# An attention and feed-forward kernel: the order of every engine and of the loads fixed by one model

## The chip, the cores, the metric

The kernel runs on one core of a Trainium2 chip. The metric is the time of one execution on the device in microseconds (us), lower is better. Medians are over repeated executions. A profile is of one execution; its span is about 2 us shorter than the time.

## The reference, cut to what matters

```python
def _attn_ref(q, k, v, n_global, n_local):      # 4 batches, 8 heads, 768 rows, 64 wide
    scores = (q @ k^T) / 8
    keep = (column < 8) | (0 <= row - column < 96)     # 8 global columns, a local band of 96
    scores = where(keep, scores - slope[head] * dist, -1e9)
    return softmax(scores) @ v

def _moe_ref(x, w_in, w_out):                   # 3072 rows, 512 -> 2048 -> 512
    h = x @ w_in
    return (h - tanh(h)) @ w_out

def reference(...):
    x = attention output, heads side by side: (3072, 512)
    return _moe_ref(x, w_in, w_out)
```

## The kernel before

The 3072 rows are 24 tiles of 128 rows, six for each batch. Every tile goes through attention (cast to bf16, transpose, scores, exp, product with a mask, product with V, normalization, transpose), then through the input matmuls with w_in (in groups of one or three tiles), tanh and subtraction, and the output matmuls with w_out. Only a band of two 128x128 blocks of scores per tile is computed; the eight global columns are copied into each tile's own K and V. That copy of V, eight partitions tall, is done on GpSimd ("the V copy").

All loads of q, k, v go through the queue of the SyncE engine (tile 0's q alone through ScalarE's), the four quarters each of w_in and w_out through GpSimd's. A planner fixes the order of TensorE, with a guess of when loads land; GpSimd's program is fixed by the place of each call. ScalarE, VectorE and SyncE are ordered by the default scheduler. The parts that the change touches:

```python
    EARLY = 3
    groups = [[0], [1], [2], [3, 4, 5]] + [[u, u + 1, u + 2] for u in range(6, NU, 3)]
    ...
    def cast(u):
        kf, qf, vf = staged.pop(u)
        ...
        eng = nc.vector if u < EARLY else nc.gpsimd
        eng.tensor_copy(out=k_bf, in_=kf.rearrange("p h d -> p (h d)"))
        eng.tensor_copy(out=q_bf, in_=qf.rearrange("p h d -> p (h d)"))
        nc.gpsimd.tensor_copy(out=vb[u % NV][:, :, 0:Dh], in_=vf)
    ...
    def a_AV(u, part):
        ...                                           # the matmuls with V, then:
        if part == 1 and 1 <= i < NQ - 1:             # the V copy
            nc.gpsimd.tensor_copy(out=vb[u % NV][0:G, :, 0:Dh], in_=vb[(u - i) % NV][0:G, :, 0:Dh])
    ...
    PRE = 3
    after = {0: [("in", 0)], 1: [("in", 1)], 2: [("in", 2), ("in", 3)],
             5: [("out", 0), ("out", 1), ("out", 2), ("out", 3)]}

    with tc.manual_schedule(engines={ENG.PE, ENG.Pool}):
        for u in range(PRE):
            load(u)
        build_masks()

        def weights(u):
            for kind, j in after.get(u, []):
                load_w(kind, j, gate=load_dma[u, "kf"])   # issued once tile u's k has landed

        weights(0)
        cast(0)
        for t, c in order:            # the planner's order of TensorE
            if c[0] == "T":           # transposes of tile u
                u = c[1]
                if u + PRE < NU:
                    load(u + PRE)
                if u + 1 < NU:
                    weights(u + 1)
                    cast(u + 1)
            ...
```

The softmax here doesn't subtract the row's maximum and nothing guards it: scores larger than these inputs give would overflow.

## Time and profile before

| | before |
|---|---|
| time, median of 3 (range) | 258.38 us (257.66 to 258.41) |
| profiled span, mean granted clock of TensorE | 256.0 us, 0.998 |
| TensorE busy, by the page | 86% |
| TensorE work done by 60 us / left after it | 26.0 us / 178.3 us |
| last quarter of w_out landed | 55.6 us |

The fourth row is a count of mine. I take the weight loads of each TensorE line up to a moment (there is one for each matmul), each counted once, at its start, and give each what such a matmul costs back to back: 0.163 us for an input matmul of 128x384, 0.109 for 128x256, 0.056 for 128x128, 0.216 for an output matmul, 0.057 for a transpose, 0.030 for the attention's small ones. In sum 204.3 us.

From the page of the kernel before: busy tenths of TensorE and of the DMA engines, and the rate moved, in 40 slices of 6.4 us; then the chain of work that ended last.

```profile
span 256.0 us, 4940 instructions
PE   1107688769999999988998799999998999999994
DMA  8999999999901959915860119811011100211012
GB/s 157 220 210 203 231 205 201 194 221 225 254 31 41 228 145 180 191 42 147 184 123 4 41 60 231 164 41 41 3 41 41 44 4 0 82 44 41 0 44 82
PE 74%; DMA 10%; DVE 5%; ACT 5%; SPq 3%; issue 1%; POOL 0%
```

In the first ten slices (64 us) the DMA engines are full and TensorE is not; in the rest it is the other way about. The longest DMA pieces of the chain (start, duration):

```profile
7.51 10.70 DMA qf<-in_q_dram
...
40.91 14.73 DMA w_out_bf_105<-in_moe_w_out_dram
```

The first is tile 2's q, until 18.2 us. The second is the last quarter of w_out, until 55.6 us. Why the first holds TensorE is seen on VectorE's timeline (start, duration, what; in brackets the idle time before it and what ended it):

```profile
9.26 0.68 DVE L174 COPY qk<-sm 128x1024 bf16<-128x1024 bf16 x1
16.10 0.43 DVE L156 CAST k_bf<-kf 128x512 bf16<-128x512 f32 x1 [6.16 <-DMA kf<-in_k_dram]
18.23 0.43 DVE L157 CAST q_bf<-qf 128x512 bf16<-128x512 f32 x1 [1.71 <-DMA qf<-in_q_dram]
18.57 0.68 DVE L191 TENSOR_TENSOR pd<-pd,mk 128x1024 bf16<-128x1024 bf16 x1
```

The mask product of tile 0 at 18.57 could have run from 11.7 us, when its exp on ScalarE ended; it stands behind the casts of tile 2, which wait for their loads. And TensorE waits for that product (waits of TensorE up to 75 us: in total, times, longest):

```profile
PE op L208 <- DVE pd L191: 9.5, 3, 8.7
```

The steady part, by stretches (columns: length, then busy us and instructions of TensorE, its weight loads, VectorE, ScalarE and GpSimd, the granted clock, the DMA share, GB/s):

```profile
60.00:100.00 40.00, 39.38 (x335) 22.67 (x333) 24.51 (x46) 19.35 (x24) 8.62 (x15) 1.00 0.65 150
100.00:140.00 40.00, 37.78 (x349) 21.57 (x348) 27.15 (x49) 20.59 (x26) 7.75 (x13) 1.00 0.61 123
140.00:180.00 40.00, 37.93 (x329) 21.50 (x328) 24.20 (x49) 16.30 (x22) 11.22 (x19) 1.00 0.42 93
180.00:220.00 40.00, 39.12 (x338) 22.17 (x337) 27.92 (x49) 22.07 (x27) 5.17 (x9) 1.00 0.08 28
```

TensorE's busy time is 154.2 of these 160 us, 96%. The counted work is 147.4 us, 92%. The Trainium skill, "Perfetto Trace Analysis", "Identifying the Most-Contended Engine", says that the busy share of matmuls is a bad measure because matmuls are pipelined, and tells the reader to look at the share of the peak reached and at the weight loads instead.

### The profile page before, as it was taken

To read this page: it belongs to the slowest core of one execution; us is meant where nothing else is said; L and a number is where in the kernel's file an instruction comes from. 1 tells how busy PE (TensorE), PEld (TensorE's weight loads), DVE (VectorE), ACT (ScalarE), POOL (GpSimd) and SP (SyncE) were. 2 spreads that over 40 slices of the span, in tenths; PEclk is the share of its full clock that TensorE was granted. 3 is DMA by queue.
4 is the path that set the end of the run, shared out by engine and by line. 5 is a ranking of instruction groups with operands and counts; after the bars stand their busy time and mean duration, and the time that the engine had idled before them with its cause. 6 is when DMAs were issued, how large, how long until landed. Compare 5 with 4: busy or idle time off the path is not lost.

```text
span 256.0 us, 4940 instructions
## 1 busy us (share of the span) xinstructions
PE 218.9 (86%) x2016; PEld 129.9 (51%) x2016; DVE 148.8 (58%) x286; ACT 113.1 (44%) x145; POOL 57.8 (23%) x107
## 2 busy tenths in 40 slices
PE   1107688769999999988998799999998999999994
PEld 0005577535555556544655366555654556545541
DVE  2223878953774558655668557744785577444710
ACT  5300556702743535651467235722582455234610
POOL 6231239241003327006200244042001500000000
PEclk9999999999999999999999999999999999999999
DMA  8999999999901959915860119811011100211012
GB/s 157 220 210 203 231 205 201 194 221 225 254 31 41 228 145 180 191 42 147 184 123 4 41 60 231 164 41 41 3 41 41 44 4 0 82 44 41 0 44 82
DMA packets 82582, 29.68 MB, mean 116 GB/s; under 512 B 75392, under 2 KB 79488, under 8 KB 82560
## 3 DMA queue, kind: packets, MB, share of 16 engines
q1 hardware_dynamic: 77296, 24.91, 44.8%
q0 software_dynamic: 4224, 4.19, 10.0%
q10 hardware_dynamic: 1040, 0.26, 0.5%
q8 instruction: 16, 0.26, 0.4%
q14 instruction: 6, 0.05, 0.1%
HBM read 27.26 MB, written 6.29 MB: 131 GB/s over the span
## 4 chain that ended last, share of the span: by engine, by line
PE 74%; DMA 10%; DVE 5%; ACT 5%; SPq 3%; issue 1%; POOL 0%
PE big L263 31%; PE op L292 30%; DMA w_out_bf_105<-in_moe_w_out_dram 6%; DMA qf<-in_q_dram 4%; PE big L182 4%; PE sm L173 3%; SPq L143 3%; PE sm L208 2%; PE sm L237 2%; ACT ot L298 2%; ACT pd L190 2%; PE sm L292 1%; PE sm L213 1%; DVE xT L242 1%; DVE pd L191 1%
## 5 line engine op out<-in xcount | busy, mean ns | idle before, releaser
L272 ACT ACTIVATE th<-big 128x768 f32<-128x768 f32 (+1 forms) x68 | 52.5, 773 | 70.1 <-PE big L263 70.1
L275 DVE TENSOR_TENSOR g<-big,th 128x768 bf16<-128x768 f32 x56 | 53.6, 956 | 21.7 <-ACT th L272 21.6
L292 PEld LDWEIGHTS <-g 128*128 128x128 bf16 x384 | 34.1, 97 | 37.5 <-issue 4.1
L298 ACT COPY ot<-op 128x512 f32<-128x512 f32 x23 | 13.5, 586 | 49.6 <-PE op L292 49.5
L190 ACT ACTIVATE pd<-big 128x1024 bf16<-128x1024 f32 x24 | 24.5, 1020 | 12.8 <-PE big L182 12.6
L292 PE MATMUL op<-w_out_bf_102,g 128*128 128x512 bf16 x92 | 23.6, 379 | 2.9 <-ACT ot L298 2.7
L208 PEld LDWEIGHTS <-pd 128*128 128x128 bf16 x192 | 14.0, 98 | 21.7 <-DVE pd L191 10.1
L263 PE MATMUL big<-xT,w_in_bf_98 128*128 128x384 bf16 (+1 forms) x160 | 24.4, 303 | 0.0
L292 PE MATMUL op<-w_out_bf_105,g 128*128 128x512 bf16 x92 | 23.8, 380 | 0.5 <-DVE g L275 0.4
L263 PE MATMUL big<-xT,w_in_bf_101 128*128 128x384 bf16 (+1 forms) x160 | 23.3, 294 | 0.7 <-ACT pd L190 0.7
L292 PE MATMUL op<-w_out_bf_103,g 128*128 128x512 bf16 x92 | 23.7, 380 | 0.3 <-DMA w_out_bf_103<-in_moe_w_out_dram 0.3
L263 PE MATMUL big<-xT,w_in_bf_99 128*128 128x384 bf16 (+1 forms) x160 | 23.3, 294 | 0.4 <-DVE g L277 0.4
L292 PE MATMUL op<-w_out_bf_104,g 128*128 128x512 bf16 x92 | 23.6, 380 | 0.0
L263 PE MATMUL big<-xT,w_in_bf_100 128*128 128x384 bf16 (+1 forms) x160 | 23.3, 294 | 0.2 <-DVE g L277 0.2
L220 DVE RECIPROCAL rden<-sm 128x4 f32<-128x4 f32 x42 | 7.6, 181 | 23.9 <-PE sm L213 21.5
L190 ACT ACTIVATE po<-big 128x1024 bf16<-128x1024 f32 x20 | 20.5, 1024 | 1.7 <-PE big L182 1.5
L191 DVE TENSOR_TENSOR pd<-pd,mk 128x1024 bf16<-128x1024 bf16 x24 | 17.2, 716 | 5.0 <-ACT pd L190 4.7
L242 DVE COPY xT<-sm 128x512 bf16<-128x512 bf16 x24 | 10.2, 423 | 15.8 <-PE sm L237 15.8
L174 DVE COPY qk<-sm 128x1024 bf16<-128x1024 bf16 x24 | 16.5, 687 | 4.6 <-PE sm L173 4.5
L182 PE MATMUL big<-qk 64*128 64x128 bf16 x352 | 16.2, 224 | 3.3 <-DVE qk L174 3.3
L221 DVE TENSOR_TENSOR x<-sm,rden 128x256 bf16<-128x256 f32 x42 | 17.8, 424 | 1.3
L263 PEld LDWEIGHTS <-w_in_bf_101 128*128 128x128 bf16 x160 | 13.7, 98 | 8.4 <-issue 0.8
(105 smaller groups left out, 249.0 us busy)
## 6 DMA issues: line engine op xcount, KB each, us to landing
kf<-in_k_dram SPq DMA_DIRECT2D x24, 256.0 KB, 5.0
vf<-in_v_dram SPq DMA_DIRECT2D x24, 256.0 KB, 4.9
out_dram<-ot SPq DMA_DIRECT2D x24, 256.0 KB, 2.0
qf<-in_q_dram SPq DMA_DIRECT2D x23, 256.0 KB, 4.9
w_in_bf_98<-in_moe_w_in_dram POOLq DMA_DIRECT2D x1, 512.0 KB, 7.6
w_in_bf_99<-in_moe_w_in_dram POOLq DMA_DIRECT2D x1, 512.0 KB, 9.0
w_in_bf_100<-in_moe_w_in_dram POOLq DMA_DIRECT2D x1, 512.0 KB, 6.2
w_in_bf_101<-in_moe_w_in_dram POOLq DMA_DIRECT2D x1, 512.0 KB, 9.3
```

Source lines behind the costliest of these rows:

```text
L174: nc.vector.tensor_copy(out=qk[u], in_=tr)
L182: nc.tensor.matmul(s[:, slot(2 * p + hh), :], qk[ku][r, 1, p, :], qk[qu][r, 0, p, :], start=True, stop=True,)
L190: nc.scalar.activation(e, s, AF.Exp, bias=0.0, scale=scale)
L191: nc.vector.tensor_tensor(out=e, in0=e, in1=mk[:, :, m, :], op=ALU.mult)
L208: nc.tensor.matmul(av[:, h, :], pd[u][:, slot(h0 + h), :], vb[u % NV][:, h0 + h, :], start=True, stop=(i == 0),)
L221: nc.vector.tensor_tensor(out=xs[u][:, h0 : h0 + H // 2, :], in0=av[:, :, 0:Dh], in1=rden.to_broadcast([P, H // 2, Dh]), op=ALU.mult,)
L242: nc.vector.tensor_copy(out=xT[g][:, :, o : o + P], in_=tr)
L263: nc.tensor.matmul(t[:, a, o : o + n], w_in_bf[j][:, c, fo : fo + P], xT[g][:, c, 0:n], start=(c == 0), stop=(c == CD - 1),)
L272: nc.scalar.activation(tv, src, AF.Tanh, bias=0.0, scale=1.0)
L275: nc.vector.tensor_tensor(out=dst, in0=src, in1=tv, op=ALU.subtract)
L292: nc.tensor.matmul(o, gs[g][:, f, t * P : (t + 1) * P], w_out_bf[f // FJ][:, f % FJ, :], start=(f == 0), stop=(f == CF - 1),)
L298: nc.scalar.copy(out=ot, in_=o)
```

## The change

Its intent: make every engine's order fit one model that knows each engine, each PSUM bank, each buffer and the DMA engines, so that no engine stands behind an instruction that cannot start. Four parts, named as in the prediction:

- (a) Order of loads: tiles 0 to 2, w_in0, tile 3, w_in1 to w_in3, w_out0, w_out1, tile 4, w_out2, w_out3, tile 5. Where tile and weight loads alternate, a gate (a wait on the landing of the load two places earlier) holds the next load back.
- (b) The k and q casts of tiles 1 and 2 go from VectorE to GpSimd.
- (c) The first groups are 2, 2, 2 tiles instead of 1, 1, 1, 3.
- (d) ScalarE, VectorE, SyncE, TensorE and GpSimd all follow the model's order.

Two small things go along: tile 0's q is loaded through SyncE's queue, and tile 3's product with V uses another PSUM tile.

```diff
-    EARLY = 3
-    groups = [[0], [1], [2], [3, 4, 5]] + ...
+    groups = [[0, 1], [2, 3], [4, 5]] + ...
...
+    before = [("t", 0), ("t", 1), ("t", 2), ("in", 0), ("t", 3), ("in", 1), ("in", 2), ("in", 3),
+              ("out", 0), ("out", 1), ("t", 4), ("out", 2), ("out", 3), ("t", 5)]
+    for n, it in enumerate(before):
+        if n >= 2 and (it[0] == "t") != (before[n - 1][0] == "t"):
+            gate_of[("ld", "kf", it[1]) if it[0] == "t" else it] = landed(before[n - 2])
...
+        e0 = DVE if u == 0 else POOL
+        op(("ck", u), e0, 0.62, lambda ...: cast(u, "k_bf", ...),
+           after=[("ld", "kf", u)], take=["kb"], give=["kf"])
+        op(("T", u), PE, 0.46, lambda ...: a_T(u),
+           after=[("ck", u), ("cq", u), ...], take=["sm"], give=["kb", "qb"])
... (one such line for each operation: engine, duration, what it follows, buffers taken and given)
     def plan():
-        T_TILE, T_W = 3.5, 3.2
-        (a model of TensorE with guessed landings)
+        (takes, again and again, the operation that can start first; loads share one DMA resource)
...
-    with tc.manual_schedule(engines={ENG.PE, ENG.Pool}):
-        (loads, weights and casts at fixed places of TensorE's order)
+    with tc.manual_schedule(engines={PE, ACT, DVE, POOL, SP}):
+        for t, key in sorted(order, key=lambda x: x[0]):
+            ops[key]["fn"]()
```

## The prediction

> **What bounds the kernel now.** By the page the span is 256.0 us. TensorE is busy 86%, but its records overlap, so I count back-to-back costs from the chain of waits: an output matmul (128x512) takes 0.216 us, an input matmul 128x384 0.163 us and 128x128 0.056 us. All of it is about 83 us of input matmuls, 83 of output matmuls and, as an estimate, 39 of attention: 205 us. The other 51 us are lost:
> - Head. The chain has 25.6 us in two DMA waits: a q load until 18.2 us, and the last quarter of w_out until 55.6 us. The DMA engines are saturated up to 60 us (table by stretches). By then TensorE has done three tiles of input matmuls and 26 of 384 output matmuls: some 26 of the 205 us.
> - Steady state, 60 to 252.5 us: about 179 us of work in 192.5 us; the rest is short steps of ScalarE and VectorE in the chain.
> - Tail, 3.5 us.
>
> **Head, in detail.** The four w_out loads are issued only at 38.7 to 40.9 us, behind about nine tiles of q, k, v, and land between 45 and 56 us, while TensorE starves. VectorE waits 6.2 us for tile 2's k with tile 0's mask product behind it (TensorE waits 8.7 us for that product).
>
> **The change.** The arithmetic stays. (a) Loads are gated into the order tiles 0-2, w_in0, tile 3, w_in1-3, w_out0-1, tile 4, w_out2-3, tile 5. (b) Casts of tiles 1 and 2 leave VectorE for GpSimd, about 0.9 us each; tile 0's attention no longer waits behind a DMA. (c) Groups 1,1,1,3 become 2,2,2: 128x256 input matmuls, estimated 0.109 us between the measured sizes, so TensorE time stays within 1 us. (d) ScalarE, VectorE and store order follow the model instead of the default scheduler.
>
> **Cost.** The DMA part (3) gives a weight quarter 3.2 us (10.0% of the span over 8); a tile costs about 3.45 us in the head. Then w_in3 lands near 29-31 us, w_out1 near 35-37, w_out3 near 45-47, tile 5 near 48-51. The Trainium skill, "DMA: Bandwidth & Descriptors", "Issuing engines are not separate DMA queues", says queues share the same engines and interleave; so ungated tiles slow the weights. The trace agrees: w_out lands 6.8 to 14.7 us after issue. I expect one small bubble: w_in1 sits on GpSimd behind a copy that waits for tile 1's attention.
>
> So by 47 us TensorE should have done four tiles of input matmuls, one of output matmuls and four to five attentions, about 25 us of work, with 10 us of output matmuls ready: from there it is busy. Before, that point came at about 57 us. Gain of the head: 9 to 11 us. Then 180 us of work, plus steady losses of 6 to 12 us (14 now), plus a tail of 3.5 us: span 236 to 242, time about 2.4 us more. Prediction 241 us.
>
> **On the critical path.** Nearly all of (a) and (b); (d) only in part, since TensorE already was 97% busy there; (c) nearly nothing.
>
> **What would show it.** Last w_out landing before 49 us; TensorE idle under 1 us per 20 us from 48 us on; input matmuls of four tiles done by 40 us; output matmuls at 60 us 60 or more (26 before); DMA in the chain under 22 us; steady ScalarE and VectorE shares of the chain halved.
>
> **What would make it wrong.** A load later than the model's, with in-order engines stuck behind it; bubbles at the gates; GpSimd casts too slow for tiles 1-3; the single output bank stalling TensorE; VectorE freeing PSUM late.

## The result, and the profile after

| | before | after |
|---|---|---|
| time, median of 3 (range) | 258.38 us (257.66 to 258.41) | 243.92 us (243.36 to 244.26) |
| profiled span, granted clock | 256.0 us, 0.998 | 242.5 us, 0.990 |
| TensorE work done by 60 us | 26.0 us | 33.5 us |
| work left after 60 us, and time for it before the tail | 178.3 in 192.5 us | 170.5 in 179.0 us |
| DMA pieces of the chain | 10% | 2% |
| last quarter of w_out landed | 55.6 us | 46.4 us |

The ratio of after to before is 0.9446, 95% interval 0.9408 to 0.9484. A ratio here and below is the mean time of one kernel's fast runs over that of the kernel before in the same rounds, so it is not quite the ratio of the medians quoted.

The span shrank by 13.5 us. By the counts of the table: 7.5 us of it is work done earlier (33.5 - 26.0), 5.7 us is less loss after 60 us (14.2 before, 8.5 after), and 0.3 us comes from slightly cheaper matmul shapes (204.0 us of work in all instead of 204.3). The tail is 3.5 us in both.

The page after, the same lines (slices of 6.06 us):

```profile
span 242.5 us, 4763 instructions
PE   1477867999999979999999999999999999999994
DMA  8997998999999998580991161101100101111112
GB/s 157 218 216 114 203 219 130 217 223 210 260 236 232 207 251 205 97 188 31 221 214 46 35 142 43 43 3 43 44 26 19 46 0 46 45 43 46 43 43 87
PE 85%; DVE 5%; ACT 3%; DMA 2%; issue 2%; SPq 1%; POOL 1%; ACTq 0%; POOLq 0%
```

Of the DMA pieces of the chain 2% of the span is left; the two long ones are gone. TensorE works from the second slice. There are two dips in the DMA rate, in the fourth and seventh slice (114 and 130 GB/s). Both are seen on GpSimd's timeline, where a weight load stands behind a V copy that waits for TensorE:

```profile
18.45 0.61 POOL L231 COPY vb_107<-vb_106 8x512 bf16<-8x512 bf16 x1 [4.39 <-PE op L212]
19.01 0.75 POOL L153 DMA_DIRECT2D w_in_bf_99<-in_moe_w_in_dram  x1
...
37.25 0.61 POOL L231 COPY vb_109<-vb_106 8x512 bf16<-8x512 bf16 x1 [10.68 <-PE op L212]
37.81 0.75 POOL L156 DMA_DIRECT2D w_out_bf_104<-in_moe_w_out_dram  x1
```

Tile 0's mask product, at 18.57 us before, now runs as soon as its exp is there, on VectorE:

```profile
8.92 0.69 DVE L196 TENSOR_TENSOR pd<-pd,mk 128x1024 bf16<-128x1024 bf16 x1 [1.83 <-ACT pd L192]
```

The stretches after:

```profile
60.00:100.00 40.00, 37.39 (x396) 24.86 (x397) 29.07 (x57) 20.09 (x24) 15.65 (x24) 1.00 1.08 230
100.00:140.00 40.00, 39.18 (x370) 23.72 (x374) 29.77 (x58) 20.20 (x26) 12.01 (x19) 1.00 0.51 114
140.00:180.00 40.00, 39.54 (x343) 23.11 (x347) 27.55 (x52) 20.15 (x25) 9.29 (x15) 1.00 0.16 46
180.00:220.00 40.00, 39.74 (x319) 23.00 (x322) 22.94 (x40) 18.99 (x24) 1.33 (x2) 1.00 0.09 34
```

Busy time is 155.9 of 160 us, 97%, one point more than before. The counted work rose from 147.4 to 152.1 us. The worst stretch is the first, 0.89 of counted work, less than before (0.95); the others are at 0.95, 0.97 and 1.00 (0.89, 0.91 and 0.94 before).

One thing in the head the prediction had not reckoned with. Here are the first input matmuls of the kernel after on TensorE, 16 at a time:

```profile
20.13 3.22 PE L263 MATMUL big<-xT,w_in_bf_98 128*128 128x256 bf16 x16 [0.63 <-DVE xT L246]
26.33 3.54 PE L263 MATMUL big<-xT,w_in_bf_99 128*128 128x256 bf16 x16
31.90 1.91 PE L263 MATMUL big<-xT,w_in_bf_100 128*128 128x256 bf16 x16 [1.25 <-ACT pd L192]
33.65 1.91 PE L263 MATMUL big<-xT,w_in_bf_101 128*128 128x256 bf16 x16
```

The first two sixteens take 3.22 and 3.54 us, the next two 1.91 (each of these times includes the tail of the last matmul): about half the rate, and 2.9 us lost. The granted clock (third number from the right) tells it for one of them only:

```profile
20.00:24.00 4.00, 3.46 (x24) 2.52 (x24) 0.92 (x3) 0.62 (x1) 3.35 (x5) 1.00 0.94 135
24.00:26.00 2.00, 0.64 (x12) 0.47 (x12) 1.79 (x4) 0.41 (x1) 1.16 (x3) 1.00 1.24 206
26.00:28.00 2.00, 1.93 (x12) 1.45 (x13) 0.90 (x2) 0.00 (x0) 0.57 (x2) 0.56 1.24 206
28.00:30.00 2.00, 2.00 (x14) 1.39 (x11) 0.00 (x0) 0.09 (x1) 0.00 (x0) 0.58 1.22 196
```

The Trainium skill, "TensorE: Matmul & The Clock Gate", Part 1, "The HAM clock gate (the 'warmup' mystery)", says that TensorE runs at half clock until it has been active for about 3.4 us, and that the window is free-running, so that runs differ. The rates agree with it: 3.22 against 1.91. Between the two sixteens TensorE was mostly idle (0.64 us busy in 24 to 26 us).

### The profile page after: what moved, and what is told of

Read it like the earlier page. It is cut to its first block, busy times and chain, and to the rows that moved or that the text cites. A ratio compares the mean times of both kernels' runs of the same rounds, so it can differ in the third digit from the quotient of the medians.

```text
span 242.5 us, 4763 instructions
## 1 busy us (share of the span) xinstructions
PE 217.6 (90%) x1926; PEld 133.8 (55%) x1952; DVE 144.9 (60%) x274; ACT 111.0 (46%) x137; POOL 66.0 (27%) x111
## 4 chain that ended last, share of the span: by engine, by line
PE 85%; DVE 5%; ACT 3%; DMA 2%; issue 2%; SPq 1%; POOL 1%; ACTq 0%; POOLq 0%
PE big L263 35%; PE op L292 32%; PE big L184 5%; PE sm L172 5%; DMA qf<-in_q_dram 2%; PE sm L207 2%; PE sm L239 2%; DVE g L282 2%; ACT ot L302 1%; PE sm L212 1%; PE sm L292 1%; SPq L147 1%; DVE x L225 1%; ACT th L275 1%; POOL q_bf L160 1%
## 5 line engine op out<-in xcount | busy, mean ns | idle before, releaser
L275 ACT ACTIVATE th<-big 128x768 f32<-128x768 f32 (+1 forms) x60 | 51.3, 855 | 84.9 <-PE big L263 83.8
L282 DVE TENSOR_TENSOR g<-big,th 128x768 bf16<-128x768 f32 (+1 forms) x60 | 60.5, 1009 | 25.0 <-ACT th L275 24.7
L192 ACT ACTIVATE pd<-big 128x1024 bf16<-128x1024 f32 x24 | 24.5, 1021 | 11.8 <-PE big L184 11.8
L160 POOL CAST k_bf<-kf 128x512 bf16<-128x512 f32 x23 | 16.4, 712 | 36.7 <-PE sm L172 23.3
L263 PE MATMUL big<-xT,w_in_bf_98 128*128 128x384 bf16 (+1 forms) x144 | 24.6, 321 | 0.6 <-DVE xT L246 0.6
L292 PE MATMUL op<-w_out_bf_102,g 128*128 128x512 bf16 x82 | 23.1, 379 | 2.2 <-ACT ot L302 1.5
L263 PE MATMUL big<-xT,w_in_bf_99 128*128 128x384 bf16 (+1 forms) x144 | 24.8, 324 | 0.0
L302 ACT COPY ot<-op 128x512 f32<-128x512 f32 x23 | 13.5, 588 | 24.1 <-PE op L292 22.4
L263 PE MATMUL big<-xT,w_in_bf_100 128*128 128x384 bf16 (+1 forms) x144 | 23.1, 308 | 1.3 <-ACT pd L192 1.3
L292 PE MATMUL op<-w_out_bf_103,g 128*128 128x512 bf16 x88 | 23.1, 379 | 0.2
L263 PE MATMUL big<-xT,w_in_bf_101 128*128 128x384 bf16 (+1 forms) x144 | 23.1, 308 | 0.1
L292 PE MATMUL op<-w_out_bf_105,g 128*128 128x512 bf16 x87 | 22.7, 379 | 0.5 <-issue 0.2
L292 PE MATMUL op<-w_out_bf_104,g 128*128 128x512 bf16 x85 | 22.5, 379 | 0.7 <-issue 0.5
L207 PEld LDWEIGHTS <-pd 128*128 128x128 bf16 x192 | 14.6, 101 | 7.7 <-DVE x L225 3.8
L263 PEld LDWEIGHTS <-w_in_bf_98 128*128 128x128 bf16 x144 | 14.1, 102 | 8.1 <-issue 0.9
L263 PEld LDWEIGHTS <-w_in_bf_99 128*128 128x128 bf16 x144 | 14.4, 103 | 6.9
L263 PEld LDWEIGHTS <-w_in_bf_100 128*128 128x128 bf16 x144 | 13.7, 98 | 8.2 <-issue 1.2
## 6 DMA issues: line engine op xcount, KB each, us to landing
kf<-in_k_dram SPq DMA_DIRECT2D x24, 256.0 KB, 4.8
qf<-in_q_dram SPq DMA_DIRECT2D x24, 256.0 KB, 4.9
vf<-in_v_dram SPq DMA_DIRECT2D x24, 256.0 KB, 4.8
out_dram<-ot SPq DMA_DIRECT2D x24, 256.0 KB, 2.1
```

The lines of the kernel that those rows point to most:

```text
L160: eng.tensor_copy(out=dst[u], in_=src.pop(u).rearrange("p h d -> p (h d)"))
L192: nc.scalar.activation(pr[u, o], s, AF.Exp, bias=0.0, scale=scale)
L207: nc.tensor.matmul(t[:, h, :], pr[u, 0][:, slot(h0 + h), :], vb[u % NV][:, h0 + h, :], start=True, stop=last,)
L263: nc.tensor.matmul(t[:, a, o : o + n], w_in_bf[j][:, c, fo : fo + P], xT[g][:, c, 0:n], start=(c == 0), stop=(c == CD - 1),)
L275: nc.scalar.activation(h_view(ths[g, f0], g), h_view(hs[g, f0], g), AF.Tanh, bias=0.0, scale=1.0)
L282: nc.vector.tensor_tensor(out=dst, in0=h_view(hs.pop((g, f0)), g), in1=h_view(ths.pop((g, f0)), g), op=ALU.subtract,)
```

## The experiments

The theory after the result had two parts. T1: the head gains because the loads come in the right order (a) and because no VectorE instruction stands behind a load (b). T2: the steady gain is VectorE's and ScalarE's order (d). Rivals: (R1) the loads hardly matter, the fixed orders do it all; (R2) the grouping pays; (R3) the loads do it all and the orders nothing. Twelve kernels ran; all gave correct results. The names beginning with b start from the kernel before, those with u and w from the kernel after, and in those the planner plans anew with the edit, unless the text says otherwise.

The medians are of all runs, the ratios of the fast ones alone: two of the four runs of b_groups and of u_casts and one of the six of w_warm and of w_casts_warm were labelled slow.

| kernel | edit | median us (range) | ratio to before, 95% interval |
|---|---|---|---|
| after | the change | 243.92 (243.36 to 244.26) | 0.9446 [0.9408, 0.9484] |
| b_loads | before, load order (a) | 266.21 (266.08 to 266.72) | 1.0297 [1.0233, 1.0361] |
| b_casts | before, casts (b) | 254.87 (254.60 to 255.14) | 0.9888 [0.9848, 0.9928] |
| b_groups | before, groups (c) | 275.48 (272.12 to 278.20) | 1.0552 [1.0446, 1.0658] |
| u_nogate | after, no gates | 243.80 (243.33 to 244.96) | 0.9434 [0.9369, 0.9498] |
| u_oldorder | after, old load order | 251.40 (249.15 to 252.26) | 0.9732 [0.9684, 0.9781] |
| u_casts | after, old casts | 242.32 (239.30 to 243.56) | 0.9313 [0.9259, 0.9368] |
| u_groups | after, old groups | 244.25 (243.08 to 244.37) | 0.9458 [0.9423, 0.9493] |
| u_default | after, old orders of two engines | 250.87 (250.34 to 251.59) | 0.9694 [0.9622, 0.9766] |
| w_warm | after, dummy matmuls | 242.36 (239.71 to 243.41) | 0.9356 [0.9308, 0.9404] |
| w_casts_warm | u_casts, dummy matmuls | 240.67 (239.19 to 242.95) | 0.9327 [0.9281, 0.9373] |
| u_lateout | after, w_out last | 255.78 (254.75 to 256.25) | 0.9929 [0.9881, 0.9977] |
| u_lateout6 | after, w_out last, tile 6 after it | 239.96 (238.99 to 241.78) | 0.9325 [0.9266, 0.9384] |

### b_loads: the order of loads alone

```diff
-        seq = [("t", 0), ("in", 0), ("t", 1), ("in", 1), ("t", 2), ("in", 2), ("in", 3),
-               ("t", 3), ("t", 4), ("t", 5), ("out", 0), ("out", 1), ("out", 2), ("out", 3)]
+        seq = [("t", 0), ("t", 1), ("t", 2), ("in", 0), ("t", 3), ("in", 1), ("in", 2), ("in", 3),
+               ("out", 0), ("out", 1), ("t", 4), ("out", 2), ("out", 3), ("t", 5)]
...
-    after = {0: [("in", 0)], 1: [("in", 1)], 2: [("in", 2), ("in", 3)],
-             5: [("out", 0), ("out", 1), ("out", 2), ("out", 3)]}
+    after = {2: [("in", 0)], 3: [("in", 1), ("in", 2), ("in", 3), ("out", 0), ("out", 1)],
+             4: [("out", 2), ("out", 3)]}
+    loads = {0: [3], 2: [4], 3: [5, 6]}
(and the gates of the kernel after)
```

> The kernel before with the load order of the change alone (gates as in the change, groups and the scheduler of VectorE and ScalarE as before). My theory: the change gains about 7 us in the head from weights that land 9 us earlier and about 6.5 us in the steady stretch from the order of VectorE and ScalarE; the load order alone should then give 250 to 254 us, last w_out quarter landing by 48 us (55.6 before), attention work done at 20 us still poor because the VectorE casts are as before. Rival 1 (order of engines is all): 257 to 259 us. Rival 2 (grouping is all): 257 to 259 us.

It got slower, 266.21 us, against the 250 to 254 us foretold. TensorE's longest wait up to 75 us:

```profile
PE sm L220 <- POOL vb L233: 9.2, 1, 9.2
```

GpSimd stood 9.8 us at the gated load of w_out2, with a V copy behind it that TensorE needed. Between 30 and 40 us TensorE was busy 2.0 of 10 us, and then worked at half clock. So the order of loads, put into the old queues as I put it, moves the blocked queue from VectorE to GpSimd. How much of the 8 us is my own placement of the loads among GpSimd's instructions this run cannot tell; it shows that the order by itself is no gain, not what a better placing would give.

### b_groups: the groups alone

```diff
-    groups = [[0], [1], [2], [3, 4, 5]] + [[u, u + 1, u + 2] for u in range(6, NU, 3)]
+    groups = [[0, 1], [2, 3], [4, 5]] + [[u, u + 1, u + 2] for u in range(6, NU, 3)]
```

> The kernel before with groups of two tiles alone. My theory: TensorE cost per tile hardly changes and the head is bound by loads, so 256 to 261 us. Rival 2 (fewer, wider matmuls and evictions are what helps): 252 us or less.

Far slower than foretold, 275.48 us, with a wide spread; the two fast runs, 272.1 and 273.7 us, are some 14 us slower than the kernel before. In the profile the first input matmul waits for two tiles, until 32.6 us, and the w_out loads, which hang on TensorE's order, are issued at 43.5 us. But the profile fell on a slow run at a granted clock of 0.944, so I read no sizes from it, and that this is the cause is not shown. By the times alone, R2 falls for the old kernel.

### u_nogate: no gates

```diff
-        g = gate_of.get(key)
+        g = None
```

The plan stays as it is, only the waits on landings go.

> The changed kernel with the planned order of every engine kept, but no gate on any load. My theory: tiles 3 to 6 load ahead of or among the weights, w_out lands 5 us or more later than 46.3 us, and the time rises to 248 to 252 us. Rival 1 (the order of the engines does it, loads hardly matter): 243 to 245 us.

No difference: 243.80 against 243.92 us; the 248 us or more of my theory are refuted. Some weights landed later, since tiles shared the DMA engines with them: the w_out quarters took 7.3 to 18.2 us from issue to landing, 5.4 to 13.0 with gates. That is what the Trainium skill, "DMA: Bandwidth & Descriptors", "Issuing engines are not separate DMA queues", leads one to expect: all queues run on the same engines and interleave. But nothing that TensorE needed was late for it. The gates do nothing here.

### u_oldorder: the old order of loads in the new plan

```diff
-    before = [("t", 0), ("t", 1), ("t", 2), ("in", 0), ("t", 3), ("in", 1), ("in", 2), ("in", 3),
-              ("out", 0), ("out", 1), ("t", 4), ("out", 2), ("out", 3), ("t", 5)]
+    before = [("t", 0), ("in", 0), ("t", 1), ("in", 1), ("t", 2), ("in", 2), ("in", 3),
+              ("t", 3), ("t", 4), ("t", 5), ("out", 0), ("out", 1), ("out", 2), ("out", 3)]
```

> The changed kernel with the load order of before (w_in between the first tiles, all w_out after tile 5), gated so that it is really kept. Theory (an early w_out is what the head gains from): last w_out lands near 50 us or later instead of 46.3, the work done at 60 us falls by 3 to 5 us and the time rises to 247 to 249 us. Rival (as the run without gates suggests, the head of the changed kernel is not bound by loads): 243 to 245 us.

251.40 us: 7.5 us slower than the change, and more than the 247 to 249 us foretold. Work done by 20 us is 2.3 us (3.7 in the change), since w_in0 and w_in1 come ahead of tiles 1 and 2; but by 30 us it is 8.7 (8.4), so the loss comes later: by 60 us it is 24.6 (33.5). Tile 3's k is issued at 23.1 us instead of 13.4, and the input matmuls of tiles 2 and 3 begin at 45.6 us instead of 39.5. And there is a second fault, GpSimd's and then TensorE's:

```profile
51.55 0.62 POOL L163 CAST vb<-vf 128x512 bf16<-128x512 f32 x1 [4.60 <-DMA vf<-in_v_dram]
...
54.85 0.19 PE L212 MATMUL sm<-vb,po 128*128 128x65 bf16 x1 [2.61 <-POOL vb L231]
```

This v is tile 6's. It has no gate, is issued among the w_out loads and lands 16 us later; the plan did not know. Behind it stand the casts of tile 7 and then the V copy (at 54.20) for which TensorE waits. It is the fault that u_lateout below has in a larger form, so the 7.5 us are not the price of the order alone. The old order with tile 6 in the list would part the two; it was not run. The edit also keeps the gates, and this order alternates between tiles and weights more often. R1 holds for the gates of the change; for the order it stays open.

### u_casts and b_casts: the casts, in the new and in the old kernel

```diff
 u_casts, from after:
-        e0 = DVE if u == 0 else POOL
+        e0 = DVE if u < 3 else POOL
 b_casts, from before:
-    EARLY = 3
+    EARLY = 1
```

> The changed kernel with the q and k casts of tiles 1 and 2 back on VectorE, everything planned anew. Theory (the plan matters, not the engine): VectorE casts are shorter (0.43 against 0.61 us) and the plan puts them where their load has landed, so 242 to 246 us. Rival (moving the casts is what frees the first attention): VectorE again sits behind tile 2's load, tile 1's attention slips by several us and the time is 248 us or more.

> The kernel before with one part of the change alone: the q and k casts of tiles 1 and 2 on GpSimd. The order of every other instruction on every engine is unchanged. Theory from the prediction (VectorE, waiting for a load, blocks the first attention): tile 0's mask product follows its exponential at 12 us instead of 18.6, x of tile 0 is transposed by 15 to 16 us instead of 21.6, but the later head still waits for w_out until 55 us, so the end moves by 0 to 3 us: 255 to 258 us. Rival (the freed head is worth much by itself): 250 to 254 us.

In the new kernel nothing is lost with the casts on VectorE again: 242.32 us. The two fast runs, 239.3 and 241.2 us, are 1.4% below the change by the ratio, but the two slow, 243.4 and 243.6 us, lie at its time, so I claim no gain. The planner puts a cast on VectorE behind the mask products that come first, so it blocks nothing.

In the old kernel the casts give 2.6 us against the median of the kernel before in the same rounds (257.51 us), 1.1% by the ratio: 254.87 us, just below the 255 to 258 us of my theory. The comparison of instruction orders shows TensorE's, ScalarE's and the loads' order unchanged, so this is the move of four casts alone. Counted work at 20 us is 4.2 us instead of 0.8, the gain that I had foretold for tile 0; by 60 us it is 28.7 instead of 26.0. A part was lost on the way. GpSimd's timeline of b_casts, and TensorE's wait for it:

```profile
26.66 0.61 POOL L157 CAST q_bf<-qf 128x512 bf16<-128x512 f32 x1 [1.61 <-DMA qf<-in_q_dram]
...
27.91 0.61 POOL L226 COPY vb<-vb 8x512 bf16<-8x512 bf16 x1
```

```profile
PE op L213 <- POOL vb L226: 4.7, 1, 4.7
```

The V copy that TensorE waits for stands on GpSimd behind tile 3's casts, which wait for their loads. The queue that stands behind a load is another now, the fault is the same.

### u_groups: the old groups in the new plan

```diff
-    groups = [[0, 1], [2, 3], [4, 5]] + ...
+    groups = [[0], [1], [2], [3, 4, 5]] + ...
```

> The changed kernel with the first groups 1,1,1,3 again. Theory: grouping is nearly neutral in the changed kernel (242 to 246 us), since both reach the same work by 60 us; it only hurt when put alone into the kernel before, where tile 1 was late. Rival: pairs are needed, 248 us or more.

244.25 us, the same as the change. With the planner the groups are neutral; R2 falls here too.

### u_default: VectorE and ScalarE ordered by the default scheduler

```diff
-    with tc.manual_schedule(engines={PE, ACT, DVE, POOL, SP}):
+    with tc.manual_schedule(engines={PE, POOL, SP}):
```

> The changed kernel with the order of TensorE, GpSimd and the load queue kept, but VectorE and ScalarE ordered by the default scheduler again. My theory: work per microsecond of TensorE from 60 to 220 us falls from 0.96 back to 0.92 and the time rises by 5 to 7 us, to 249 to 251 us. Rival 3 (loads do it all): 243 to 245 us.

250.87 us, as foretold, and 7 us slower than the change: taking VectorE's order out costs as much as half of the whole gain. The comparison of instruction orders shows the orders of TensorE, GpSimd and SyncE unchanged and ScalarE's different by one swap only, so it is VectorE's. The chain that ended last:

```profile
PE 76%; DVE 11%; ACT 6%; DMA 2%; issue 2%; SPq 1%; POOL 1%; ACTq 0%; POOLq 0%
```

VectorE is 11% of the chain, 5% in the change. Work done by 60 us is 31.1 us (33.5 in the change), and from 60 to 220 us it is 147.2 us, the sum of the kernel before (147.4) and not that of the change (152.1). So without VectorE's order none of the steady gain is left in the sum, and 2.4 us of the head's go too. Stretch by stretch it is not the kernel before: from 60 to 100 us it does 0.84 of counted work (before 0.95), after that 0.93 to 0.96 (before 0.89 to 0.94). R3 falls.

### w_warm and w_casts_warm: a warm clock

About 70 dummy matmuls of the identity into PSUM tiles that are written afterwards anyway, where TensorE waits in the head. Core of the edit (results are unchanged by it):

```diff
+    WARM_T = {0: (24, 4), 1: (6, 8), 2: (8, 0)}     # before the transposes of k and q, by tile
+            for _ in range(WARM_T.get(u, (0, 0))[1 - j]):
+                nc.tensor.transpose(tr[u][:, j, 0, :], ident, ident)
...                                                  # likewise before scores, 5 before the first m1
```

> The changed kernel with some 70 dummy matmuls of the identity put into the idle time of TensorE in the first 20 us, results unchanged. Theory: the first 32 input matmuls (0.20 us each instead of 0.109, granted clock 0.56 to 0.58 at 26 to 30 us) run at full rate, TensorE gains 3 us in the head, of which 1 to 3 us reach the end: 241 to 243 us. Rival (hidden behind the waits for loads): 243.5 to 244.5 us.

> A version meant to beat both: the changed kernel with the casts of tiles 1 and 2 on VectorE (planned anew) and more dummy matmuls in the idle time of TensorE up to 23 us. If the two gains are of different causes they add: 238 to 241 us, mean granted clock 0.995 or more in every run, and no pair of separate time levels as in the run with fewer dummies. If they overlap: 241 to 243 us.

In the profiled run all input matmuls of the head now run at the full rate, and the first start earlier:

```profile
18.41 1.91 PE L272 MATMUL big<-xT,w_in_bf 128*128 128x256 bf16 x16 [0.37 <-DVE xT L253]
```

By its fast runs w_warm is about 1% faster than the change (0.9356 against 0.9446, the intervals just do not meet). Its times fall on two levels: 239.7 and 239.8 us, and 242.4 to 243.4 us (the last slow). The lower ones had a mean granted clock of 0.991 and 1.0, the higher ones 0.978 to 0.992. That half-rate time parts the levels, and that the dummies take it away in a part of the runs, fits this but is not shown: the clocks overlap, and only a run of the lower level has a profile. u_casts, without dummies, spreads as widely (239.3 to 243.6 us). w_casts_warm joins u_casts and more dummies: 240.67 us, with runs from 239.2 to 243.0 us. The time is as foretold, the granted clock of 0.995 or more in every run is not (0.986 to 1.0). It beats the change by about 1.3% (0.9327 against 0.9446, the intervals do not meet), but so do the two fast runs of u_casts alone (0.9313): a gain of the dummies on top of it is not seen.

### u_lateout and u_lateout6: does w_out have to come early?

Tiles 4 and 5 before all of w_out. In u_lateout6 tile 6 is added to the end of the list, so that its load, too, has a gate behind w_out, and the planner knows that it comes late.

```diff
 u_lateout:
     before = [("t", 0), ("t", 1), ("t", 2), ("in", 0), ("t", 3), ("in", 1), ("in", 2), ("in", 3),
-              ("out", 0), ("out", 1), ("t", 4), ("out", 2), ("out", 3), ("t", 5)]
+              ("t", 4), ("t", 5), ("out", 0), ("out", 1), ("out", 2), ("out", 3)]
 u_lateout6:
+              ("t", 4), ("t", 5), ("out", 0), ("out", 1), ("out", 2), ("out", 3), ("t", 6)]
```

> The changed kernel with all w_out quarters gated behind tiles 4 and 5 (w_in and tiles 0 to 3 as in the change). Theory (issuing w_out before tiles 4 and 5 is a part of the head's gain): w_out0 lands near 40 us instead of 32.4 and w_out3 near 49 instead of 46.3; 1 to 4 us slower than the change, 245 to 248 us, and the 7.5 us of the run with the whole old load order come for the larger part from tiles 1 and 2 being late. Rival (w_out is what matters): 249 us or more.

u_lateout: 255.78 us, 12 us slower than the change, where 1 to 4 had been foretold. On its own this looks as if the early w_out were worth 12 us. But TensorE's timeline does not show it waiting for w_out:

```profile
44.34 0.40 PE L172 MATMUL sm<-ident,k_bf 128*128 128x128 bf16 x4 [2.94 <-POOL k_bf L160]
50.74 0.61 PE L172 MATMUL sm<-ident,q_bf 128*128 128x128 bf16 x4 [6.00 <-POOL q_bf L160]
...
53.20 3.49 PE L263 MATMUL big<-xT,w_in_bf 128*128 128x256 bf16 x16
```

It waits for the casts of tile 6, and GpSimd for tile 6's loads:

```profile
43.67 0.61 POOL L160 CAST k_bf<-kf 128x512 bf16<-128x512 f32 x1 [5.12 <-DMA kf<-in_k_dram]
50.07 0.61 POOL L160 CAST q_bf<-qf 128x512 bf16<-128x512 f32 x1 [5.78 <-DMA qf<-in_q_dram]
```

Tile 6 is issued at about 33 us without a gate, and shares the DMA engines with w_out; the model, which serves loads one after the other, expected it sooner. So TensorE's order has its transposes at a place where they are 9 us too early, and ready matmuls stand behind them. After the gap, the 16 input matmuls at 53.20 run at half rate (3.49 us). From that reading I foretold u_lateout6:

> Like u_lateout, but tile 6 is gated behind the w_out quarters too, so that the plan knows when it lands and does not put its transposes ahead of ready work. In u_lateout TensorE stood 9 us before tile 6's transposes (its k and q shared the DMA engines with w_out) and then ran 32 matmuls at half clock. Theory (the 12 us of u_lateout are that stall, a landing that the plan did not foresee; a later w_out alone costs little): 245 to 249 us, and no TensorE wait over 3 us on a cast of tile 6. Rival (late w_out itself costs it): 252 us or more with w_out3 landing no later than 50 us.

239.96 us, 16 us better than u_lateout and 4 us better than the change, by one more entry in a list. The 245 to 249 us of my theory were too high; its sign was right:

```profile
34.44 2.97 POOL L156 DMA_DIRECT2D w_out_bf<-in_moe_w_out_dram  x4
...
50.54 0.61 POOL L160 CAST k_bf<-kf 128x512 bf16<-128x512 f32 x1 [3.25 <-DMA kf<-in_k_dram]
```

Tile 6's k is cast at 50.54, later than in u_lateout (43.67). But now the plan knew, and TensorE had other work first: its longest wait for a GpSimd cast up to 75 us is 1.1 us. Counted work by 60 us is 34.9 us (33.5 in the change, 24.4 in u_lateout). w_out lands from 40.3 to 48.8 us, later than in the change (32.4 to 46.4 us), and the kernel is no slower for it.

It is the fastest kernel by the median; by the ratios it cannot be told from w_casts_warm and u_casts. Its lead over the change is 1.3% by the ratios, with intervals that do not meet. Of its 4 us I can assign no shares; tile 6 in the change's own list, with w_out early, was not run. In its head only the first sixteen input matmuls are slow; GpSimd casts tile 3's k and q at 21.24 and 21.79 us, where in the change the q is cast behind a V copy at 25.40; the mean granted clock of most of its runs is 1.0 against 0.99; and the stretch from 80 to 100 us is at 0.98 of counted work, 0.86 in the change. The plan differs in all three at once.

## Why the prediction was right, and where it was not

The number was right: 241.0 us foretold, 243.92 measured, inside the 238.4 to 244.4 us that its span of 236 to 242 us and 2.4 us give.

1. **The sum.** The prediction's point from which TensorE is busy was 47 us, with about 25 us of work done; the trace has 24.5 us of work at 50 us. Work from there: 180 us foretold, 179.5 counted (204.0 - 24.5). Losses from there: 6 to 12 us foretold, 9.5 counted (239.0 - 50 - 179.5). The tail is 3.5 us as foretold. So the mis-sized term is the head, "9 to 11 us", and 7.5 by the count at 60 us. It is about 3 us late, and 2.9 us is what two sixteens of input matmuls lost at half clock: the prediction costed every matmul at its warm, back-to-back price. That this is all of the lateness is argued from the sizes; w_warm, where the dummies worked, gives it support (239.7 us).

2. **The signs.** Last w_out before 49 us: true, 46.4. DMA in the chain under 22 us: true, about 5 (2%). Output matmuls at 60 us: 60 or more foretold, 46 by the count of weight loads (27 before by the same count). False; about 3 us of output matmuls (14 of them) is the lateness under 1. Input matmuls of four tiles by 40 us: false, 49.7. TensorE idle under 1 us per 20 us from 48 us on: false from 60 to 100 us, where it was busy 37.4 of 40 us; true in sum from there on. ScalarE and VectorE in the chain halved: false over the whole span (5% and 5% before, 5% and 3% after); from 140 to 220 us they are all but gone.

3. **The step that failed.** The prediction put on the critical path "Nearly all of (a) and (b); (d) only in part, since TensorE already was 97% busy there; (c) nearly nothing." Only the last held in the planned kernel. The sum was made of stretches and not of these shares, so the right number does not vouch for them.
   - (d) is worth as much as half of the gain: without VectorE's order the kernel is at 250.87 us, 7 us slower. "97% busy" was read from a column that is busy by records, not by work. The same text counted 14 us of steady loss, which that column hides, and its own sum took 2 to 8 us of it away. I had the better number and argued with the worse one.
   - (a) stays open in size. The old order of loads costs 7.5 us in the plan (u_oldorder), but tile 6's unplanned landing is in that number. The gates are worth nothing (u_nogate), and early w_out is not needed (u_lateout6), though the 14.73 us wait for w_out was the longest piece of the chain of the kernel before.
   - (b) alone gave about 3 us in the old kernel, and in the new one the engine of the casts is indifferent: what counts is that the cast is placed behind what is ready.
   - (c) neutral in the plan, harmful without it.

4. **What ties it together.** The long TensorE gaps that I followed, other than the wait for the first loads and that for the last w_out of before, show the same picture: an in-order queue stands at an instruction that waits for a load, and what TensorE needs is ready behind it. VectorE in before, 8.7 us. GpSimd in b_casts, 4.7 us, and in b_loads, 9.2 us. GpSimd in u_oldorder, 2.6 us. TensorE itself in u_lateout, 2.9 and 6.0 us. That the gain of the change is to lay out all queues for the landings that then come is my reading of all these runs together; the pair u_lateout and u_lateout6 is its best test. The prediction named this among what would make it wrong ("A load later than the model's, with in-order engines stuck behind it") but did not see that the same thing is why the change works, and why its parts are worth nothing or less by themselves: +8 us for the loads, some +14 us for the groups, about -3 us for the casts, where the whole is -14.5 us.

5. **What stays open.** How the 7.5 us of the head divide between the load order and the plan: the parts are not additive, so the question may have no answer. What the old load order costs when the plan knows of tile 6. Why the change does less work from 60 to 100 us than the kernel before (0.89 against 0.95). Why w_warm has two levels. What b_loads would give with the best placing of its loads on GpSimd. Which part of u_lateout6's 4 us is the clock.

## What to carry to other kernels

Where queues are in order, a load's place and the places of all instructions that wait for it are one decision: change them together, and expect half a change to cost. The longest DMA wait of a chain need not be the one to shorten; ask first what else the engine could do meanwhile, as u_lateout and u_lateout6 show (16 us apart, by one entry that let the plan know of a late load). And judge TensorE by counted work against back-to-back cost, with the matmuls after each gap looked at for half rate, not by its busy share.

## What the Trainium skill lacked or had wrong

- "TensorE: Matmul & The Clock Gate", Part 1, says that the warm-up costs under 1% of a typical kernel's span. That holds here for one warm-up, but not for the kernel: it had two, sixteen input matmuls each, at 3.22 and 3.54 us instead of 1.91, together 2.9 us or 1.2% of 242.5 us.
- The same page warns that a trace's clock events are not to be fully trusted. It does not say that the granted clock of the profile may read full before the first record of a change. It read 1.00 from 20 to 24 us, where sixteen matmuls took 3.22 us; the record has 0.56 only from 26 us. The rate of equal matmuls is the safer sign, and the mean granted clocks above can leave out such time (u_lateout6's profiled run has 1.0 with its first sixteen at 3.57 us).
- "SBUF — State Buffer", "SBUF: two separate sides", says that a VectorE instruction with two SBUF inputs and a GpSimd instruction that reads SBUF lock a port pair against each other for the whole instruction. The trace after agrees: GpSimd's cast at 8.92 us took 1.17 us instead of 0.62, beside VectorE's mask product of 0.69 us that began at the same time. It gives no size for a whole kernel: here GpSimd's 23 casts of k had a mean of 0.71 us, since five took 1.01 to 1.11 us, against a median of 0.62, so about 0.1 us each.
- "Perfetto Trace Analysis" has VectorE, ScalarE and GpSimd as strictly first in, first out, but I found no page that warns of the instruction that waits for a load with ready work behind it. It made the gaps of 8.7, 4.7 and 9.2 us here, and 9 us on TensorE.
